# Another order in the opening of a fused attention and gated-MLP kernel, and its transposing transfers issued apart

## The chip, the cores and the metric

The kernel runs on one core of a Trainium2 chip. The metric is the device time of one execution in microseconds. A core has five engines that run side by side, each with a queue of its own that is worked off in order: TensorE (PE, the matrix products, with PEld its weight loads), VectorE (DVE), ScalarE (ACT), GpSimd (POOL) and SyncE (SP, which here only issues transfers). ScalarE and GpSimd also issue some transfers. Sixteen DMA engines carry them out.

## The reference

```python
x  = A_x                                   # 2048 rows of 1024, bf16
xn = layernorm(x)                          # (x - mean) / sqrt(var + 1e-5)
q, k, v = split(xn @ wqkv)                 # 32 heads of 32
# each row attends to 8 rows: itself and 2, 4, ... 14 rows back (masked before row 0)
s  = softmax(q . k[s - 2w] * 32**-0.5) . v[s - 2w]
s  = s @ wo
b  = (silu(xn @ w1) * (xn @ w3)) @ w2      # 3584 hidden columns
out = x + s * silu(b)
```

## The kernel before

The 2048 rows are four chunks of 512 (`CH`), handled in two blocks `b` of two chunks. Each of the large products of a block (`qkv`, the two up-projections, the down-projection, `wo`) is done with fewer products than its size asks for: sums and differences of blocks of operands are formed on VectorE (`xn_sums`, `qkv_sums`, `w_sums`, `w2_sums`, `wo_sums`), multiplied on TensorE, and put together from PSUM by ScalarE (copies, helper `cp`, line 447) and VectorE (additions, helper `tt`, line 442). Every product goes through `mm` (line 433). Two smaller helpers for products of 256 columns are at lines 1008 and 1267.

The code does not issue instructions in the order in which it is written. Each step becomes an `Op` of a `Plan` with an engine, cells that it reads and writes, and a cost. `Plan.depend` derives who follows whom from the cells, `Plan.limits` gives each a due time, counted back from the fixed order of TensorE, and `Plan.simulate` goes through time with a cost model and lets each engine take, of the steps that are ready, the one that is due first. The result is the order of instructions on each queue. `plan.nudge` shifts single due times by hand (the name of a step and its occurrence), and `plan.rows` fixes the order of the opening by hand: one list each for VectorE, ScalarE and SP. The waits in the program come from the tiles that instructions touch, not from the cells.

**Opening.** TensorE first does twelve products on zeros (line 406). SP loads the four row groups of chunk 0 (`x0_0` to `x0_3`, 256 KB each), those of chunk 1 (`x1_...`), and the weights of `q` and `k` in halves (`wqkv0_0` in two pieces `a` and `b`, `wqkv0_1`, `wqkv1_0`, `wqkv1_1`; 1 MB a half). VectorE takes the statistics of each group (`bn`, `ba`, lines 512 and 515), ScalarE the root (`sq`, line 517), VectorE the reciprocal (`rc`) and the normalising (`ts`, line 520). Group 2 of chunk 0 takes its statistics on ScalarE instead (`ln_mix`, lines 553 to 562). TensorE then transposes a normalised group by eight products with a unit matrix (`ln_tp`, line 585; called `tp` below), and ScalarE copies them to `xT` (line 592). In `rows0`, `q` of chunk 0 is computed for each row group as soon as it is there (`part`), with products on zeros between (`idle_mm`, line 572). `k` follows (`qkv_first` with `mid`): four products groups on `wqkv1_0`, with the transposing of a group of chunk 1 after each.

**Chunks 2 and 3.** Their rows are normalised on ScalarE alone in `mlp_down(0)` (`ln_act`: `mean`, `var`, `sq`, then `nrm` at line 544) and transposed by DMA: `ln_td` (line 601) issues one transposing transfer for each row group, eight in all, from ScalarE's queue.

**Around them, in `mlp_down`.** `pa`, `pb` and `pe` are PSUM banks of the three streams. ScalarE makes the gates (`gsilu`, step `dg`, line 450), the copies `dfork`, `dsu`, `dsp` and, at 256 columns, `dq21`, `dq5`, `dq2`. VectorE adds with `dq12`, `dq22`, `dsb`, `dsa`. TensorE may write a bank `pe[g]` in the second half only after `dsp` has copied it. `dsb` reads the product that then follows.

**Attention** runs on VectorE as filling work beside the products: `qk`, `qa`, `qb`, `qc`, then a softmax (`z`, `tr`, `zd`; the exponential on ScalarE at line 866 with a table load of its own), then `pv`, `pa`. Attention of a chunk lasts over many product steps.

Of the kernel before, what the change touches and what calls it, by code (L numbers as in the profile page):

```python
# [14 lines left out]
PE, DVE, ACT, POOL, SP = range(5)  # L15
# [39 lines left out]
class Plan:  # L55
# [105 lines left out]

    def hop(self, a, b):
        if a.nbytes:
            return 0.1
        if a.eng == PE:
            return 0.0 if b.eng == PE else 0.25
        return 0.05
# [25 lines left out]
    def simulate(self):  # L193
        ops = self.ops
        free = [0.0] * 5
        ready = [[] for _ in range(5)]
        pes = [o.idx for o in ops if o.eng == PE]
        pe_at = 0
        table = None
        ring = {e: [] for e in (SP, ACT, POOL)}  # L200
        now = 0.0
        for o in ops:
            o.n, o.ready = len(o.pred), 0.0
            o.start = None
        for o in ops:
            if not o.n and o.eng != PE:
                ready[o.eng].append(o.idx)
        order = []

        def landed(until):  # L210

            nonlocal now
            while True:
                heads = [r[0] for r in ring.values() if r]
                live = [h for h in heads if h[0] <= now + 1e-9]
                step = min([h[0] for h in heads if h[0] > now + 1e-9] + [until])
                if live:
                    total = sum(h[2] for h in live)
                    dt, e = min((h[1] * total / h[2], h[3].eng) for h in live)
                    end = now + dt <= step  # L220
                    dt = dt if end else step - now
                    if dt > 0.0:
                        for h in live:
                            h[1] -= dt * h[2] / total
                    if end:
                        now += dt
                        return ring[e].pop(0)[3]
                now = max(now, step)
                if step >= until:
                    return None  # L230

        def release(o, queued, data):
            for s in o.succ:
                q = ops[s]
                if (o.idx, s) in self.queued:
                    if not queued:
                        continue
                elif not data:
                    continue
                else:  # L240
                    at = o.done + self.hop(o, q)
                    if o.nbytes and q.eng != PE:
                        at += max(0.0, min(self.SPARE * (1 if o.run > 256 else 4), 0.5 * (q.limit - q.lift - at)))
                    q.ready = max(q.ready, at)
                q.n -= 1
                if not q.n and q.eng != PE:
                    ready[q.eng].append(s)

        while len(order) < len(ops):
            best = None  # L250
            for e in reversed(range(5)):
                if e == PE:
                    if pe_at == len(pes) or ops[pes[pe_at]].n:
                        continue
                    T = max(free[PE], ops[pes[pe_at]].ready)
                elif ready[e]:
                    T = max(free[e], min(ops[i].ready for i in ready[e]))
                else:
                    continue
                if best is None or T < best[0]:  # L260
                    best = T, e
            o = landed(best[0] if best else 1e9)
            if o:
                o.done = now + self.TAIL
                release(o, False, True)
                continue
            T, e = best
            if e == PE:
                o = ops[pes[pe_at]]
                pe_at += 1  # L270
            else:
                i = min((i for i in ready[e] if ops[i].ready <= T), key=lambda i: (ops[i].limit, i))
                ready[e].remove(i)
                o = ops[i]

            occ = o.occ
            if o.table and o.table != table:
                occ += 1.29
                table = o.table
            o.start = T  # L280
            free[e] = T + occ
            order.append(o)
            if o.nbytes:
                ring[e].append([T + self.LAG[e], self.work(o), self.share(o), o])
                release(o, True, False)
            else:
                o.done = T + occ + o.lat
                release(o, True, True)
        while any(ring.values()):
            o = landed(1e9)  # L290
            o.done = now + self.TAIL
        self.order = order
        return order
# [13 lines left out]
def kernel(  # L307
# [93 lines left out]
    warm = plan.pools["k2"][7][:].bitcast(BF16)  # L401
# [9 lines left out]
    def bank(name):  # L411
        return plan.slot("mm", name)
# [49 lines left out]
    def xt_cells(half, kh, st=None):  # L462
        return [("xT", half, (kh * KH + k) * 2 + q // 2, q % 2) for k in range(KH)
                for q in (range(4) if st is None else [st])]
# [101 lines left out]
    def idle_mm(n):  # L566

        ps = bank("idle")

        def emit():  # L570
            for _ in range(n):
                nc.tensor.matmul(ps.ap(), lhsT=ident[:], rhs=zero, start=True, stop=True)

        plan.op(PE, "idle", emit, [], [ps], n * MM, 0.0)
# [23 lines left out]
    def ln_td(c, st, xt):  # L598

        half = c % 2  # L600
        plan.op(ACT, f"td{c}_{st}", lambda: nc.scalar.dma_start_transpose(  # L601
            out=xT[:, half, :, st * P:(st + 1) * P], in_=xrow(xt, st)),
            [(xt, st)], xt_cells(half, 0, st) + xt_cells(half, 1, st), 1.3, 0.0, nbytes=256 * 1024, run=256)

    def qkv_load(t, pieces=1):
        wts = []
# [82 lines left out]
    def qkv_first(nm, wts, mid=None, rows=None):  # L689

        pa = [bank(f"f{nm}{j}") for j in range(4)]
        def part(st, ks=range(KH)):
            for j in range(4):
                mm(pa[j], [qkv_w(wts[0], k, j) for k in ks], [bx[0, 0][k] for k in ks], st == 0 and ks[0] == 0,
                   wk_cells(wts[0], ks) + xt_cells(0, 0, st), st=(st, 1))

        if rows:
            rows(part)
        for j in range(4):
            if mid is not None and j:  # L700
                mid(j - 1)
            if not rows:
                mm(pa[j], [qkv_w(wts[0], k, j) for k in range(KH)], bx[0, 0], True, wk_cells(wts[0]) + xt_cells(0, 0))
            dst, wr = first_at(nm, j)
            cp("fsnap", dst, pa[j].ap, [pa[j]], wr)
        for j in range(4):
            if mid is not None and j == 0:
                mid(3)
            mm(pa[j], [qkv_w(wts[1], k, j) for k in range(KH)], bx[0, 1], False, wk_cells(wts[1]) + xt_cells(0, 1))
            dst, wr = home(0, nm)(j)  # L710
            cp("fc11", dst, pa[j].ap, [pa[j]], wr)
# [815 lines left out]
    for st in range(NST):  # L1527
# [1 line left out]
    plan.op(ACT, "warm", lambda: nc.scalar.activation(out=scr[:], in_=eps_t[:], func=ACTF.Sqrt), [], [], 0.2,  # L1529
            table="sqrt")  # L1530
    plan.rows = [row.split() for row in (
# [6 lines left out]
    )]  # L1538
    plan.rank = {n: i for row in plan.rows for i, n in enumerate(row)}
    for st in range(NST):  # L1540
# [3 lines left out]
    plan.rows += [["ts1_3", f"w2s{i}"] for i in range(FH // 2)]  # L1544
    plan.rows += [["wqkv2_1", f"w2q{i}"] for i in range(5, FH // 2)]
    plan.nudge = {
# [4 lines left out]
    }  # L1551
    ln_dve(0, 0, x0)
    ln_mix(0, 2, x0)
# [2 lines left out]

    def rows0(part):
        ln_tp(0, 0, x0)
        idle_mm(4)
        part(0, (0, 1))  # L1560
        ln_tp(0, 2, x0)
        idle_mm(2)
        part(0, (2, 3))
        part(2)
        ln_tp(0, 1, x0)
        ln_tp(0, 3, x0)
        part(1)
        part(3)
# [98 lines left out]
```

## Time and profile before

| | us |
|---|---|
| runs, median of 3 (lowest to highest) | 714.8 (714.68 to 715.42) |
| the profiled execution, its own time | 714.41 |
| span of that execution | 712.6 |
| busy, of the span: PE, DVE, ACT, POOL | 704.3, 687.4, 411.2, 38.6 |

The span reaches from the first to the last instruction; what is outside it is start and end. Busy time of TensorE is counted from the start of a product to its modelled end, so that a wait shorter than the pipeline does not show. In the rows of the profile L433 is a line of the program, `mm<-xs,r` what is written and read (buffer numbers left out), `x16` how many instructions a row merges, and a bracket at the end gives the idle time of the engine ahead of the row and what ended it. "issue" means that nothing in the profile ended the wait. ACTq and SPq are the queues of ScalarE and SP.

The granted clock of TensorE in the execution is 0.999.

### The profile page before, as it was taken

The page shows a single profiled execution, that of the slowest core. Times are in us where ns is not written, and L with a number is a line of the kernel's source. Part 1 is how long each engine was busy: PE and PEld are TensorE (multiplying, and loading weights), DVE is VectorE, ACT ScalarE, POOL GpSimd, SP SyncE. Part 2 cuts the span into 40 slices and gives each one's busy share as a digit, 9 for nine tenths or more (in the row PEclk, how much of TensorE's full clock was granted, in tenths as well). Part 3 has the DMA queues.
Part 4 walks back from the last instruction along what each step waited for, and adds up shares of the span by engine and source line. Part 5 has one row for each costly group of instructions (what it writes and reads, how often), then busy time and mean ns, then how long its engine had stood idle before and what let it go on. Part 6 is the DMA issues. An engine that isn't in the chain of part 4 may idle for free.

```text
span 712.6 us, 9970 instructions
## 1 busy us (share of the span) xinstructions
PE 704.3 (99%) x3634; PEld 369.1 (52%) x3634; DVE 687.4 (96%) x959; ACT 411.2 (58%) x762; POOL 38.6 (5%) x78
## 2 busy tenths in 40 slices
PE   8999999999999999999999999999999999999997
PEld 5655555555555544644555555544555554465443
DVE  7998999999999999999999999998999999999967
ACT  7744466668766796622635355668665764431333
POOL 0010111001200000000100000000000000100000
PEclk9999999999999999999999999999999999999999
DMA  9879987567865768797724569979656654646633
GB/s 326 324 282 324 316 301 237 207 209 265 258 210 174 244 219 210 208 277 267 249 86 168 178 189 354 326 251 287 218 168 233 183 169 156 188 135 230 228 142 104
DMA packets 132241, 162.13 MB, mean 228 GB/s; under 512 B 13280, under 2 KB 109152, under 8 KB 126688
## 3 DMA queue, kind: packets, MB, share of 16 engines
q1 hardware_dynamic: 117776, 127.35, 55.5%
q0 software_dynamic: 5824, 31.99, 12.0%
q10 hardware_dynamic: 8592, 2.16, 1.7%
q8 instruction: 28, 0.46, 0.3%
q14 instruction: 21, 0.17, 0.1%
HBM read 112.72 MB, written 38.27 MB: 212 GB/s over the span
## 4 chain that ended last, share of the span: by engine, by line
PE 56%; DVE 1%; ACT 1%; ACTq 1%; issue 0%; DVEq 0%
PE mm L433 51%; PE mm L1008 3%; PE mm L1267 2%; DVE r L442 1%; ACTq L601 1%; ACT k L447 0%; ACT L866 0%; ACT L450 0%; ACT h_sb L450 0%; ACT att L866 0%; DVEq L1662 0%; ACTq L866 0%; DVEq L442 0%
## 5 line engine op out<-in xcount | busy, mean ns | idle before, releaser
L433 PEld LDWEIGHTS <-r 128*128 128x128 bf16 (+1 forms) x2064 | 217.9, 108 | 195.9 <-issue 1.5
L433 PE MATMUL mm<-xs,r 128*128 128x512 f16 x1056 | 251.4, 379 | 0.2 <-ACT k L447 0.2
L433 PE MATMUL mm<-xT,r 128*128 128x512 bf16 (+1 forms) x1008 | 232.3, 369 | 0.9 <-ACT k L447 0.5
L447 ACT COPY k<-mm 128x512 f32<-128x512 f32 (+1 forms) x256 | 132.9, 535 | 58.8 <-PE mm L433 44.0
L433 PE MATMUL mm<-r,h_sb 128*128 128x512 bf16 (+1 forms) x704 | 154.1, 379 | 1.1 <-ACT k L447 1.1
L433 PEld LDWEIGHTS <-h_sb 128*128 128x128 f16 (+1 forms) x800 | 78.3, 98 | 94.8 <-issue 1.3
L442 DVE TENSOR_TENSOR att<-att 128x1024 bf16<-128x1024 bf16 (+6 forms) x176 | 104.7, 610 | 3.7 <-ACT att L866 2.5
L447 ACT COPY mm<-mm 128x512 f32<-128x512 f32 (+1 forms) x120 | 62.1, 520 | 55.9 <-PE mm L433 41.7
L442 DVE TENSOR_TENSOR att<-qo,kT 128x2048 bf16<-128x2048 bf16 x64 | 78.0, 1226 | 3.7 <-ACT kT L447 2.9
L450 ACT ACTIVATE k<-k 128x512 bf16<-128x512 f32 x56 | 33.2, 625 | 62.9 <-DVE k L442 62.9
L442 DVE TENSOR_TENSOR att<-E,vT 128x2048 bf16<-128x2048 bf16 x56 | 66.9, 1223 | 0.0
L442 DVE TENSOR_TENSOR r<-r,r 128x256 f16<-128x256 f16 (+7 forms) x99 | 64.0, 663 | 0.7 <-PE mm L433 0.4
L442 DVE TENSOR_TENSOR h_sb<-mm,k 128x1024 bf16<-128x1024 f32 (+1 forms) x56 | 61.2, 1108 | 0.1
L1008 PEld LDWEIGHTS <-r 128*128 128x128 f16 x392 | 38.3, 98 | 28.3
L450 ACT ACTIVATE h_sb<-mm 128x512 bf16<-128x512 f32 x60 | 35.9, 601 | 18.9 <-PE mm L433 18.8
L442 DVE TENSOR_TENSOR k<-mm,k 128x1024 f32<-128x1024 f32 (+1 forms) x44 | 45.2, 1029 | 1.1 <-PE mm L433 1.0
L1008 PE MATMUL mm<-xT,r 128*128 128x256 f16 x224 | 42.8, 273 | 0.0
L447 ACT CAST k<-mm 128x512 bf16<-128x512 f32 x56 | 32.5, 586 | 15.6 <-PE mm L433 15.4
L442 DVE TENSOR_TENSOR h_sb<-h_sb 128x1024 f16<-128x1024 bf16 (+3 forms) x51 | 39.3, 804 | 0.1
L442 DVE TENSOR_TENSOR qo<-qo,att 128x2048 bf16<-128x2048 bf16 x32 | 39.2, 1224 | 0.1
L442 DVE TENSOR_TENSOR r<-r 128x1024 f16<-128x1024 bf16 (+2 forms) x64 | 36.8, 581 | 0.0
L442 DVE TENSOR_TENSOR h_sb<-h_sb,k 128x2048 bf16<-128x2048 bf16 x28 | 34.3, 1225 | 0.3 <-ACT k L447 0.3
(107 smaller groups left out, 511.7 us busy)
## 6 DMA issues: line engine op xcount, KB each, us to landing
r<-in_B_w_dram SPq DMA_DIRECT2D x42, 512.0 KB, 4.9
s_dram<-r POOLq DMA_DIRECT2D x14, 1024.0 KB, 5.4
r<-t_dram SPq DMA_DIRECT2D x16, 896.0 KB, 6.9
r<-s_dram SPq DMA_DIRECT2D x14, 1024.0 KB, 5.5
r<-in_A_wqkv_dram SPq DMA_DIRECT2D x11, 1024.0 KB, 7.7
r<-in_B_w_dram SPq DMA_DIRECT2D x12, 896.0 KB, 4.8
h_sb<-in_B_w_dram SPq DMA_DIRECT2D x14, 512.0 KB, 11.1
t_dram<-h_sb POOLq DMA_DIRECT2D x7, 1024.0 KB, 6.9
```

The costliest lines, as they stand in the source:

```text
L433: nc.tensor.matmul(cut(ps.ap()), lhsT=lhs[k](), rhs=cut(rhs[k]()), start=(first and k == 0), stop=(last and k == n - 1), skip_group_check= ...
L442: plan.op(DVE, name, lambda: fn(out=o(), in0=a(), in1=b()), rd, wr, occ, 0.08, late=late)
L447: plan.op(ACT, name, lambda: nc.scalar.copy(out=o(), in_=a()), rd, wr, occ, 0.11)
L450: plan.op(ACT, name, lambda: nc.scalar.activation(out=o(), in_=a(), func=ACTF.Silu), rd, wr, occ, 0.11, table="silu")
L601: plan.op(ACT, f"td{c}_{st}", lambda: nc.scalar.dma_start_transpose(out=xT[:, half, :, st * P:(st + 1) * P], in_=xrow(xt, st)), [(xt, st)] ...
L1008: nc.tensor.matmul(ps.ap()[:, h * 256:(h + 1) * 256], lhsT=lhs[k](), rhs=rhs[k](), start=first and k == 0, stop=False, skip_group_check=True)
L1267: nc.tensor.matmul(ps.ap()[:, col * 256:(col + 1) * 256], lhsT=lhs[k](), rhs=r()[:, k, :], start=first and k == 0, stop=False, skip_group_ ...
```

## The change

Three parts.

1. The planner: a transposing transfer now also writes a cell `"turned"`, so that the planner puts the eight one behind the other. `hop` lets such a transfer follow 1.4 us before the planner's landing of the last, and the planner's spare time for landings is left out there.
2. The opening: `x0_3` is loaded ahead of the weights, `x1_1` ahead of `wqkv0_1`; two products on zeros instead of six; `part(2)` in two halves around `tp0_1`; VectorE's first statistics of group 1 go ahead of the reciprocal of group 0, and `qs2` (one of the sums of weights) goes from behind group 0 to behind `ts1_1`; ScalarE's roots and copies are ordered to match. In `qkv_first`, the first transposing of chunk 1 goes ahead of the first products of `k`, the next two ahead of the third and the fourth.
3. Other nudges, which shift due times of steps throughout.

```diff
     def hop(self, a, b):
         if a.nbytes:
-            return 0.1
+            return -1.4 if a.run == b.run == 256 and a.eng == b.eng == ACT else 0.1
...
-                    if o.nbytes and q.eng != PE:
+                    if o.nbytes and q.eng != PE and at > o.done:
...
         plan.op(ACT, f"td{c}_{st}", lambda: nc.scalar.dma_start_transpose(
             out=xT[:, half, :, st * P:(st + 1) * P], in_=xrow(xt, st)),
-            [(xt, st)], xt_cells(half, 0, st) + xt_cells(half, 1, st), 1.3, 0.0, nbytes=256 * 1024, run=256)
+            [(xt, st)], xt_cells(half, 0, st) + xt_cells(half, 1, st) + ["turned"], 1.3, 0.0, nbytes=256 * 1024, run=256)
...
         for j in range(4):
-            if mid is not None and j:
-                mid(j - 1)
+            if mid is not None and j != 1:
+                mid(max(j - 1, 0))
...
     plan.rows = [row.split() for row in (
-        "bn0_0_0 bn0_0_1 ba0_0 rc0_0 ts0_0 bn0_1_0 rc0_2 ts0_2 bn0_1_1 bn0_3_0 ba0_1 bn0_3_1 rc0_1 ba0_3 ts0_1 rc0_3 ts0_3 "
-        "bn1_0_0 bn1_0_1 ba1_0 qs2 bn1_1_0 bn1_1_1 rc1_0 ts1_0 ba1_1 bn1_2_0 bn1_2_1 rc1_1 ts1_1 ba1_2 bn1_3_0 rc1_2 ts1_2 "
-        "bn1_3_1 ba1_3 rc1_3 ts1_3 qs0 qs1 xs0 qs3 xs1",
-        "warm mean0_2 sq0_0 var0_2 sq0_2 xT0_0_0 xT0_0_1 xT0_2_0 sq0_1 xT0_2_1 sq0_3 xT0_1_0 xT0_3_0 xT0_1_1 xT0_3_1 fsnap "
+        "bn0_0_0 bn0_0_1 ba0_0 bn0_1_0 rc0_0 ts0_0 bn0_1_1 rc0_2 ba0_1 ts0_2 bn0_3_0 bn0_3_1 rc0_1 ba0_3 ts0_1 rc0_3 ts0_3 "
+        "bn1_0_0 bn1_0_1 ba1_0 bn1_1_0 bn1_1_1 rc1_0 ba1_1 ts1_0 bn1_2_0 rc1_1 bn1_2_1 ts1_1 qs2 ba1_2 bn1_3_0 bn1_3_1 "
+        "rc1_2 ba1_3 ts1_2 rc1_3 ts1_3 qs0 qs1 xs0 qs3 xs1",
+        "warm mean0_2 sq0_0 var0_2 sq0_2 xT0_0_0 sq0_1 xT0_0_1 xT0_2_0 sq0_3 xT0_2_1 xT0_1_0 xT0_1_1 xT0_3_0 xT0_3_1 fsnap "
         "sq1_0 sq1_1 sq1_2 sq1_3",
-        "x0_0 x0_2 x0_1 wqkv0_0a x0_3 wqkv0_0b x1_0 wqkv0_1 x1_1 x1_2 wqkv1_0 x1_3 wqkv1_1",
+        "x0_0 x0_2 x0_1 x0_3 wqkv0_0a wqkv0_0b x1_0 x1_1 wqkv0_1 x1_2 wqkv1_0 x1_3 wqkv1_1",
     )]
...
     plan.nudge = {
-        ("wu0", 2): 10.01, ("w3.4", 0): -20.17, ("wu0", 4): 8.99, ("ws0", 5): -6.56, ("uq12", 6): 9.09, ("ws1",
...
+        ("wu0", 2): 10.01, ("w3.4", 0): -16.78, ("wu0", 4): 8.98, ("ws0", 5): -12.22, ("uq12", 6): 9.09, ("ws1",
...
     def rows0(part):
         ln_tp(0, 0, x0)
-        idle_mm(4)
+        idle_mm(2)
         part(0, (0, 1))
         ln_tp(0, 2, x0)
-        idle_mm(2)
         part(0, (2, 3))
-        part(2)
+        part(2, (0, 1))
         ln_tp(0, 1, x0)
+        part(2, (2, 3))
         ln_tp(0, 3, x0)
```

6 rows, old and new, of the table table are left out of this document.

## The prediction

> **What bounds the kernel now.** I read the busy shares first, then the stages, then the waits. In the stage rows the columns are: stretch, its length, the busy time and count of PE, PEld, DVE, ACT and POOL, the granted clock, the DMA share and GB/s.
>
> ```profile
> PE 704.3 (99%) x3634; PEld 369.1 (52%) x3634; DVE 687.4 (96%) x959; ACT 411.2 (58%) x762; POOL 38.6 (5%) x78
> ```
> ```profile
> 66.00:260.00 194.00, 194.00 (x998) 99.83 (x997) 193.55 (x300) 132.25 (x254) 20.63 (x38) 1.00 0.72 243
> 260.00:303.00 43.00, 41.87 (x243) 23.65 (x242) 42.87 (x59) 30.52 (x50) 0.99 (x2) 1.00 0.79 216
> 303.00:484.00 181.00, 181.00 (x872) 94.64 (x870) 178.98 (x229) 90.08 (x164) 6.15 (x12) 1.00 0.74 235
> ...
> 497.00:685.00 188.00, 188.00 (x979) 95.74 (x978) 186.67 (x222) 93.54 (x175) 5.46 (x10) 1.00 0.59 191
> ```
>
> TensorE is full nearly everywhere, and VectorE is just as full: 193.55 of 194 us from 66 to 260, 178.98 of 181 from 303 to 484. Time can come only from the few holes, and where VectorE has none, TensorE cannot run ahead for long. The waits name the holes.
>
> ```profile
> PE mm L433 <- ACT k L447: 1.8, 3, 1.1
> ```
> ```profile
> ACT L450 <- issue: 5.8, 1, 5.8
> ACT r L544 <- issue: 5.5, 1, 5.5
> ```
>
> TensorE waits 1.8 us for copies of ScalarE (line 447), and ScalarE twice sits idle over 5 us with no releaser, only "issue". The transposing transfers (line 601) explain that. Of the eight issues the shortest, the median and the longest, in ns, and then ScalarE at the longest wait of TensorE (ACTq is its queue, which issues):
>
> ```profile
> L601 ACTq DMA_TRANSPOSE xT<-r x8: 1247/1600/6474, 264.6 to 301.4; - x8
> ```
> ```profile
> 292.17 0.38 ACT L447 COPY k<-mm 128x256 f32<-128x256 f32 x1
> ...
> 294.84 1.25 ACTq L601 DMA_TRANSPOSE xT<-r  x1
> 294.97 0.38 ACT L447 COPY k<-mm 128x256 f32<-128x256 f32 x1
> 296.18 3.65 ACTq L601 DMA_TRANSPOSE xT<-r  x1
> 299.88 0.58 ACT L447 COPY k<-mm 128x512 f32<-128x512 f32 x1 [4.53 <-PE mm L1267]
> ```
> ```profile
> 297.69 0.93 PE L1267 MATMUL mm<-r,xs 128*128 128x256 f16 x7
> 298.45 0.93 PE L1267 MATMUL mm<-r,xT 128*128 128x256 f16 x7
> 300.51 3.83 PE L433 MATMUL mm<-r,h_sb 128*128 128x512 bf16 x17 [1.13 <-ACT k L447]
> ```
> ```profile
> 303.73 0.69 DVE L442 TENSOR_TENSOR k<-mm,k 128x512 f32<-128x512 f32 x1 [0.76 <-PE mm L433]
> ```
>
> An issue alone takes 1.25 us; one right behind another takes 3.65, and the copy `dsp` queued behind it starts at 299.88, when the queue is free again. TensorE needs that copy before it may overwrite the bank. Seven products of 256 columns take 0.76 us from start to start (297.69 to 298.45), so the next product was due at 299.21 and came at 300.51: **1.30 us** lost. VectorE then stands 0.76 us at its next product-fed addition (`dsb`).
>
> **The change part by part.**
>
> *Transposes one by one.* The new cell "turned" binds each to the one before it in the planner only; no instruction gets a wait from it. In the changed order of ScalarE the first of the second four stands ahead of the last two 128x256 copies, the second behind them, the third behind the four `dsp`, the last behind the first gate. So the second follows the first by two copies and their waits. It is still ahead of `dsp`. ScalarE's queue reaches the first at about 292.3 (the copy ahead of it, `dq5`, started at 292.17, and the queue runs ahead of its engine), and the second at about 295, where the second small copy ran (294.97). From 294.84 to the end of the following issue, 299.83, the first needed 4.99 us to make room: 292.3 + 5.0 = 297.3. The `dsp` copy then starts at about 297.3, ends at 297.9, and the bank is free before 299.21. Gain on TensorE 1.30; on VectorE 0.76, because it goes on without the hole. The price of the first transpose ahead of two copies that TensorE needs through VectorE is between nothing and 1.25 us; I take nothing, as those copies were held by the normalising pass (line 544) before, which now stands ahead of them.
>
> *Opening.* All of VectorE's and TensorE's work up to 17.8 us ends in a wait for a load of weights:
>
> ```profile
> 5.55 0.16 DVE L519 RECIPROCAL small<-small 128x1 f32<-128x1 f32 x1 [0.49 <-ACT small L517]
> ...
> 6.21 0.69 DVE L512 BATCH_NORM_STATS2 small<-r 128x6 f32<-128x512 bf16 x1
> ```
> ```profile
> 6.81 1.03 PE L572 MATMUL mm<-E,ident 128*128 128x512 bf16 x4
> 7.67 0.65 PE L433 MATMUL mm<-xT,r 128*128 128x128 bf16 x8
> ...
> 16.69 0.81 PE L433 MATMUL mm<-xT,r 128*128 128x512 bf16 x3
> 17.82 1.08 PE L433 MATMUL mm<-xT,r 128*128 128x512 bf16 x4 [0.32 <-DMA r<-in_A_wqkv_dram]
> ...
> 20.06 0.61 PE L585 MATMUL mm<-ident,r 128*128 128x128 bf16 x8
> 20.51 0.82 PE L433 MATMUL mm<-xT,r 128*128 128x512 bf16 x3
> ```
> ```profile
> 2.00:16.00 14.00, 13.55 (x123) 9.22 (x122) 11.65 (x28) 10.32 (x25) 0.15 (x2) 1.00 0.99 363
> ```
>
> SP's loads ahead of the end of `wqkv1_0` stay the same 4.75 MiB (seven of x at 256 KB, three MiB of weights), on DMA engines that are full (a share of 0.99), so I keep 17.82 for it. Four products on zeros less are 4 x 0.215 (6.81 to 7.67) = 0.86 us of TensorE, hidden under loads: `wqkv0_0a` now follows `x0_3`, and the second part of `q` needs `wqkv0_0b`, whose place is unchanged. They are worth nothing by themselves. VectorE's first statistics of `x0_1` (0.6 us; a row of one lasts 0.69, pipelined) go into the hole of 0.49 from 5.06 (0.49 ahead of 5.55) and stand ahead of `rc0_0` and `ts0_0`, which everything on TensorE waits for. The trace shows only that `x0_1` was there at 6.21; so these two come between 0.1 (rows there at 5.06) and 1.26 us later; I take 0.45. `x1_1` ahead of `wqkv0_1` delays these weights by 256 KB, 0.7 us at 363 GB/s. TensorE ended `q` at 17.34 (16.69 and three products of 0.215); with fewer zeros and rows earlier I put it at 16.85, and between 16.7 and 17.34. What counts is behind it: the first transposing by products of chunk 1 (`tp1_0`) now stands ahead of the products on `wqkv1_0`, so it runs inside the wait before 17.82. It costs 20.06 to 20.51, **0.45 us**, which leaves the path; TensorE would be ready at 17.3, with 0.52 to spare, and even from 17.34 it would just be in time. On VectorE, `qs1` overwrites chunk 1 only after the last such transposing, so it gains the same 0.45. Nothing stands between that and the point where attention starts:
>
> ```profile
> 65.94 1.23 DVE L442 TENSOR_TENSOR att<-qo,kT 128x2048 bf16<-128x2048 bf16 x1 [2.91 <-ACT kT L447]
> ```
>
> VectorE waits there for a copy that TensorE feeds, so both carry 0.45 to 299.
>
> *Nudges.* Between 18 and 66 only one exchange of ScalarE's copies, at 44, is new. VectorE's order from 66 to 484 differs by exchanges of neighbours, one product of attention put off from 260 to 281, and the sums of 323 to 333 in another order. In 259 to 262 a product with the gate now follows copies that end close ahead of it: I count 0.1 us of idle VectorE, between 0 and 0.3. Two loads change places with a neighbour. All are behind full engines and cost nothing, if their readers are not late.
>
> *Where the lead is spent.* TensorE is then 1.75 us early at 303 and VectorE 0.45 + 0.76 - 0.1 = 1.11. From there to 484 VectorE has no hole left, and at 484 ScalarE's exponential stops TensorE:
>
> ```profile
> 482.89 1.27 DVE L442 TENSOR_TENSOR att<-att 128x128 f32<-128x128 f32 x3
> ```
> ```profile
> 483.81 0.58 ACT L447 CAST k<-mm 128x512 bf16<-128x512 f32 x1 [0.28 <-PE mm L433]
> 484.42 1.28 ACT L866 ACT_TABLE_LOAD   x1
> ```
> ```profile
> 489.25 1.02 PE L433 MATMUL mm<-xT,r 128*128 128x512 bf16 x4 [0.50 <-ACT k L447]
> ```
>
> Its operand leaves VectorE at 484.16 (482.89 + 1.27), and ScalarE was free at 484.39. With ScalarE 1.75 early and VectorE 1.11, VectorE decides: 483.05 instead of 484.39, 1.34 early. The other 0.4 us of TensorE's lead turn into a longer wait before 489. Behind it TensorE has no hole to 685, so 1.34 reaches the end.
>
> **Sum.** 0.45 (opening) + 0.76 (VectorE's hole) - 0.1 (nudges) + 0.23 (margin at 484) = 1.34. The profiled execution took 714.41 (span 712.6, 1.8 outside): 713.07. The median of the runs, 714.8, is 0.39 above it, so 713.46; I say **713.4**. Were TensorE alone the bound, 1.75 would be saved: 713.05.
>
> **The rivals.**
>
> *The weights land earlier.* By bytes, 363 GB/s over 14 us are 5.08 MB by 16.0, and 4.98 MB stand up to the end of `wqkv1_0`; TensorE got it at 17.82. So a late piece, not the bytes, made the last microsecond, and it may fall elsewhere. TensorE would start at 17.3: 0.5 more, **712.9**. Against it: the queue's order is nearly the same.
>
> *The transposes still block.* If an issue is long because the shared DMA engines are loaded, spacing the issues does nothing, the `dsp` copy is late again and VectorE's hole stays: only 0.45 is left, 713.96 and with the 0.39 **714.4**. The DMA busy share in tenths, 294 to 308 in 40 slices, speaks for both:
>
> ```profile
> DMA  0000058799999999999999799999999999990009
> ```
>
> From 295.75 on the engines were busy with another load, so the first transpose may have been slow for that alone. But up to there nothing moved: issued at 292.3, the first finds them free before the second comes. The Trainium skill, "DMA: Bandwidth & Descriptors", section "Issuing engines are not separate DMA queues", says that the queues share 16 engines and an issue is usually small beside its transfer. By that rule a queue of transposes would not hold ScalarE and spacing would gain only the opening. The 3.65 against 1.25 us speak against it.
>
> *Slower: TensorE's clock falls to half in the opening*, since the products on zeros that keep it busy are fewer. Before it is warm its first twelve products take 4.74 us, 0.4 each against 0.215 later:
>
> ```profile
> 1.22 4.74 PE L406 MATMUL mm<-k 128*128 128x512 bf16 x12 [1.22 <-DVE k L403]
> ```
>
> A cold stretch of T delays the opening by T/2 less the 0.52 spare. It eats all 1.34 at T = 3.7 us; one stretch as long as the first gives 715.0, two give **717.0**. Against it: the holes that I find are up to 0.9 us (5.96, the end of the row above, to 6.8), and the 1.3 us at 299 left the granted clock at 1.00. The Trainium skill, "TensorE: Matmul & The Clock Gate", section "What's actually happening", wants an idle window of about 3.4 us for a fall; by it this rival would be dead.
>
> **How the numbers follow.** Forecast 0.50, early weights 0.20, still blocked 0.16, cold clock 0.07; 0.07 is left for stalls that I do not see in the reordered stretches, mostly a few tenths slower. A measurement of this kernel tells about 0.2% from no change, 1.43 us: the line is at 713.37, through the middle of the forecast (itself 713.0 to 713.9). So faster is 0.20 and half of 0.50, 0.45; slower 0.09, the cold clock with part of the rest; the same 0.46. The range reaches from early weights with VectorE no bound (0.95 + 1.30 saved, 712.55, rounded to 712.4) past the blocked case to 715.0, one cold stretch.
>
> **What would show it.** Right: issues on line 601 near 1.25 us, above all no 3.65 ahead of `dsp`; no hole of TensorE at 299 nor of VectorE at 303; TensorE still starting on `wqkv1_0` at 17.8, with the transposing before it; a wait before 489 that has grown to about 1 us. Wrong: a TensorE hole at 289 or 296 (small copies held by the first transpose), a pace of 0.4 us a product after 6, or no growth of the wait at 489, which would free VectorE of being the bound.

## The result, and the profile after

The runs of one measurement had a median of 714.56 us before (713.97 to 715.68, 12 runs) and 712.86 us after (712.61 to 713.93, 12 runs): a ratio of **0.9979, with a 95% interval of 0.9971 to 0.9986**, so between 1.0 and 2.1 us less. The forecast was 713.4 in a range of 712.4 to 715.0. The profiled execution took 712.69 us with a span of 710.9, 1.7 less than the span of before. The interval stays below 1, so the gain is clear of noise. The prediction's line of 0.2% lies at 713.13 for this median of before: the median is beyond it, a little, and the interval reaches across it, to 713.56.

The page of the profile after: TensorE is busy 1.4 us less, and VectorE 0.6 us less.

```profile
PE 702.9 (99%) x3630; PEld 368.7 (52%) x3630; DVE 686.8 (97%) x959; ACT 412.5 (58%) x762; POOL 38.6 (5%) x78
```

The stage in which the gain was expected, with the columns as before:

```profile
260.00:303.00 43.00, 43.00 (x250) 24.21 (x248) 42.90 (x59) 32.01 (x50) 1.11 (x2) 1.00 0.88 227
```

TensorE was busy 41.87 of these 43 us before; now it has no gap. The waits of TensorE in the profile after (what waits, for what; total, times, longest):

```profile
PE mm L585 <- DVE r L520: 1.6, 1, 1.6
PE mm L406 <- DVE k L403: 1.2, 1, 1.2
PE mm L433 <- ACT k L447: 0.7, 2, 0.5
```

The wait for ScalarE's copies fell from 1.8 to 0.7 us. In the opening the wait of TensorE's first transposing for VectorE's normalising grew from 0.4 to 1.6 us, in part because the products on zeros ahead of it ended 0.4 us earlier in this trace. First the issues of the transposing transfers (shortest, median, longest in ns), then ScalarE around the second four of them, in the timeline after:

```profile
L601 ACTq DMA_TRANSPOSE xT<-r x8: 1247/1296/4752, 263.3 to 303.1; - x8
```
```profile
291.59 1.25 ACTq L601 DMA_TRANSPOSE xT<-r  x1
291.76 0.38 ACT L447 COPY k<-mm 128x256 f32<-128x256 f32 x1
...
294.24 0.37 ACT L447 COPY k<-mm 128x256 f32<-128x256 f32 x1 [0.99 <-PE mm L1267]
294.24 1.25 ACTq L601 DMA_TRANSPOSE xT<-r  x1
296.53 0.59 ACT L447 COPY k<-mm 128x512 f32<-128x512 f32 x1 [1.92 <-PE mm L1267]
```

The two issues are 2.65 us apart and take 1.25 us each; the wide copy starts at 296.53, as soon as its product is there, instead of 3.35 us later. A long issue is left (4.75 us, at 268), but there ScalarE has room. TensorE after, at the place of the old hole, and VectorE's next product-fed addition:

```profile
297.86 0.93 PE L1267 MATMUL mm<-r,xT 128*128 128x256 f16 x7
298.62 4.70 PE L433 MATMUL mm<-r,h_sb 128*128 128x512 bf16 x21
```
```profile
302.36 0.69 DVE L442 TENSOR_TENSOR k<-mm,k 128x512 f32<-128x512 f32 x1
```

From 297.86 to 298.62 are 0.76 us, the pace of seven such products: no hole. TensorE starts there 1.89 us earlier than before (300.51), VectorE 1.37 (303.73), and its bracket of 0.76 is gone. Now the opening: TensorE's first transposing before, then TensorE and VectorE after.

```profile
6.36 0.62 PE L585 MATMUL mm<-ident,r 128*128 128x128 bf16 x8 [0.39 <-DVE r L520]
```
```profile
7.14 0.62 PE L585 MATMUL mm<-ident,r 128*128 128x128 bf16 x8 [1.59 <-DVE r L520]
...
9.19 1.24 PE L433 MATMUL mm<-xT,r 128*128 128x128 bf16 x16
...
17.18 0.61 PE L585 MATMUL mm<-ident,r 128*128 128x128 bf16 x8
17.71 1.95 PE L433 MATMUL mm<-xT,r 128*128 128x512 bf16 x8
```
```profile
5.74 0.70 DVE L512 BATCH_NORM_STATS2 small<-r 128x6 f32<-128x512 bf16 x1 [0.82 <-DMA r<-in_A_x_dram]
```

The moved transposing (17.18) runs ahead of the products on the weights of `k` (17.71). But VectorE's hole was not filled; it grew from 0.49 to 0.82, since the statistics that were moved into it wait for a load. Last, the small hole at 41 that every trace has. The product behind it, before and after:

```profile
41.74 1.46 PE L433 MATMUL mm<-xs,r 128*128 128x512 f16 x6 [0.18 <-ACT k L447]
```
```profile
41.17 2.10 PE L433 MATMUL mm<-xs,r 128*128 128x512 f16 x9 [0.16 <-ACT k L447]
```

I use the start of this product as a mark. It splits a run into an **opening** (up to the mark) and a **rest** (the run's time less the mark). Before: 41.74 and 672.67; after: 41.17 and 671.52. In these two executions the opening gave 0.57 us and the rest 1.15.

### The profile page after: what moved, and what is told of

It reads as the page before. It is cut to its first block, busy times and chain, and to the rows that moved or that the text cites. A ratio compares the mean times of both kernels' runs of the same rounds, so it can differ in the third digit from the quotient of the medians.

```text
span 710.9 us, 9963 instructions
## 1 busy us (share of the span) xinstructions
PE 702.9 (99%) x3630; PEld 368.7 (52%) x3630; DVE 686.8 (97%) x959; ACT 412.5 (58%) x762; POOL 38.6 (5%) x78
## 3 DMA queue, kind: packets, MB, share of 16 engines
q10 hardware_dynamic: 8592, 2.16, 2.1%
## 4 chain that ended last, share of the span: by engine, by line
PE 97%; DVE 1%; ACT 1%; DMA 1%; issue 0%; SPq 0%; DVEq 0%; ACTq 0%
PE mm L433 87%; PE mm L1008 6%; PE mm L1267 3%; DVE r L442 1%; DMA r<-in_A_x_dram 1%; PE mm L585 1%; ACT k L447 0%; ACT L866 0%; ACT L450 0%; SPq L456 0%; DVE small L512 0%; ACT h_sb L450 0%; DVE r L520 0%; PE mm L572 0%; ACT att L866 0%
```

## The experiments

All medians stand beside the runs of before on the same chip; a ratio is given where a kernel had more than one run. "Mark" and "rest" are of the one profiled execution. Where an expectation says "at 41", it counts from the start of the hole, 0.32 to 0.35 us ahead of the mark, so its times less that start are larger by as much.

| kernel | median (runs) | before | ratio, 95% interval | mark | rest |
|---|---|---|---|---|---|
| before | 714.56 (12) | | | 41.74 | 672.67 |
| after | 712.86 (12) | 714.56 | 0.9979, 0.9971 to 0.9986 | 41.17 | 671.52 |
| e1, opening alone | 714.48 (11) | 714.68 | 0.9996, 0.9987 to 1.0005 | | |
| e2, one transposing ahead | 714.53 (11) | 714.68 | 0.9999, 0.9990 to 1.0008 | 41.34 | 672.57 |
| e3, without the opening | 713.21 (11) | 714.68 | 0.9981, 0.9972 to 0.9989 | 42.22 | 671.48 |
| e4, one transpose moved | 714.01 (11) | 714.68 | 0.9988, 0.9980 to 0.9997 | 41.66 | 672.96 |
| e5, back to back again | 714.58 (10) | 714.45 | 0.9998, 0.9989 to 1.0007 | 40.93 | 672.68 |
| e6, fuller opening | 713.33 (11) | 714.45 | 0.9984, 0.9975 to 0.9993 | 42.50 | 671.37 |
| e7, VectorE later | 715.01 (1) | 714.45 | | 42.37 | 672.64 |
| e8, no zeros | 712.91 (1) | 714.45 | | 41.34 | 671.57 |
| e9, products earlier | 712.82 (11) | 714.25 | 0.9979, 0.9970 to 0.9988 | 41.56 | 671.34 |
| e10, opening alone again | 714.75 (1) | 714.25 | | 42.18 | 672.57 |

### e5: the two transfers back to back again

The changed kernel with one move on ScalarE:

```diff
-dq21 dq5 [td3_0] dq2 dq2 [td3_1] dsp dsp dsp dsp
+dq21 dq5 dq2 dq2 [td3_0] [td3_1] dsp dsp dsp dsp
```

> The changed kernel with one instruction moved: the first of the second four transposing transfers goes behind the two small copies, so that the first two are issued back to back again, as before the change; nothing else differs. Theory that the pair alone makes the hole: the second issue takes 3 to 4 us, the wide copies wait for it, TensorE has a hole of 1.0 to 1.3 us ahead of 299 and VectorE one of 0.5 to 0.8 at 302; the wait of TensorE at 336 for VectorE goes, as TensorE is no longer ahead; 0.9 to 1.2 us slower than the changed kernel from 42 us to the end. Rival, the loaded DMA engines make the long issue: the issue takes 1.25 to 2 us here too and nothing is lost.

Its ScalarE and TensorE at the place:

```profile
293.99 0.37 ACT L447 COPY k<-mm 128x256 f32<-128x256 f32 x1 [1.16 <-PE mm L1267]
294.06 4.82 ACTq L601 DMA_TRANSPOSE xT<-r  x2
298.92 0.58 ACT L447 COPY k<-mm 128x512 f32<-128x512 f32 x1 [4.55 <-PE mm L1267]
```
```profile
297.61 0.93 PE L1267 MATMUL mm<-r,xT 128*128 128x256 f16 x7
299.55 3.61 PE L433 MATMUL mm<-r,h_sb 128*128 128x512 bf16 x16 [1.01 <-ACT k L447]
```

The row merges both issues, 4.82 us; alone on line 601 they are 1.25 and 3.53. The wide copy starts 0.04 after their end, and TensorE's hole is back: 299.55 - 297.61 - 0.76 = 1.18. The rest goes from 671.52 to 672.68, **1.16 worse**, all that the rest had gained. One point missed: TensorE's wait at 336 stays, since VectorE falls behind as well (it waits 0.57 us at 302.77 and 0.47 at 305.79).

So putting the pair back together is enough to make the hole. Loaded DMA engines alone do not make an issue long: from 294 to 296 us the DMA share was 0.09 before, where the second issue took 3.65, and 1.02 after, where it took 1.25. The packets of the transposing transfers (DMA queue q10 on the page, 2.16 MB, which is their eight times 256 KB) show more. Where the second issue came right behind the first, the first packet moved 3.4 us after the first issue (before: 294.84, then 298.25; e5: 294.06, then 297.43); where it did not, 1.6 us after it (after the change: 291.59, then 293.20). Why a pair starts so late is not shown. The Trainium skill ("DMA: Bandwidth & Descriptors", section "Issuing engines are not separate DMA queues") expects an issue to be usually small beside its transfer; the 3.53 us here, for transfers that land 6.1 and 8.6 us after their issue, do not fit that.

### e3: without the opening; e4: one transfer moved

e3 is the changed kernel with `plan.rows`, `rows0` and `mid` of before. e4 is before with one move on ScalarE, and the orders of all other engines unchanged:

```diff
-nrm3_2 dq2 nrm3_3 dq2 [td3_0] [td3_1] dsp
+nrm3_2 dq2 [td3_0] nrm3_3 dq2 [td3_1] dsp
```

> The changed kernel with the old opening: new issue order and new nudges alone. TensorE theory: the hole ahead of 300 is gone (1.30), a wait of TensorE for VectorE at 336 takes back about 0.17, so 1.1 to 1.3 saved against before, span 711.3 to 711.5. Rival, VectorE is the bound from 303 to 484 (the forecast): 0.76 - 0.1 + 0.23 = 0.9 saved, span 711.7, and the wait of TensorE before 489 grows by 0.4. Rival, the transposes still block: nothing saved.

> Before, with one instruction moved: the first of the second four transposing transfers is issued one normalising pass and one small copy earlier on ScalarE; every other engine's order is that of before. Theory that the back-to-back issue alone made the hole: no issue over 2.5 us ahead of the four wide copies, no hole of TensorE ahead of 300, TensorE 1.3 early at 303, and 1.0 to 1.3 saved at the end (TensorE theory) or 0.76 + 0.23 = 1.0 (VectorE bound, the forecast). Rival, the issue is long since the DMA engines are loaded: the second issue still takes 3 us or more and nothing is saved. Rival, the nudges make the gain: nothing or little here.

e3: the rest is 671.48, 1.19 less than before, and the same as that of the changed kernel. That is inside the 1.1 to 1.3 of the TensorE theory and above the 0.9 that the forecast makes of this part.

e4 is not what either theory said. The second issue is short (1.25 us at 294.75, only 0.27 us behind the end of the first), and the hole at 299 is gone, but another has come ahead of it. ScalarE, TensorE and VectorE of e4:

```profile
293.23 1.25 ACTq L601 DMA_TRANSPOSE xT<-r  x1
...
294.53 1.24 ACT L544 ACTIVATE r<-r,small 128x1024 bf16<-128x1024 bf16 x1 [0.67 <-issue]
294.75 1.25 ACTq L601 DMA_TRANSPOSE xT<-r  x1
```
```profile
296.08 0.92 PE L1267 MATMUL mm<-r,xT 128*128 128x256 f16 x7 [0.66 <-ACT k L447]
```
```profile
326.73 1.23 DVE L442 TENSOR_TENSOR h_sb<-r,r 128x2048 f16<-128x2048 bf16 x1 [0.82 <-DMA r<-in_A_wo_dram]
```

The first issue holds the last normalising pass by 0.67 us and with it the small copy behind; TensorE loses 0.82 there instead of 1.30. The planner's order avoids that: after the change all four passes are done when the first transfer is issued (291.59). Then VectorE waits 0.82 for the weights of `wo`, which no other trace here does, and TensorE loses 0.83 at 337. That makes this execution's rest 0.29 worse than before. The median of its runs, 0.9988 of that of before, says that most executions gained something. Why the load was late in the profiled one was not tried.

### e7: VectorE made late

Before, with one addition on VectorE done twice (`qc1`, 128x512, at 341.5).

> Before, with one addition of VectorE (128x512, 0.34 us from start to start) done twice at 341.5; the result is the same. Theory that VectorE had room there (it met TensorE's products at 344 to 346 and waited about 0.25 us in all): 0.05 to 0.15 late at 347, and nothing at the end. Rival, VectorE has no room from 303 to 484 (the forecast's picture): 0.34 late at 347 and still so at 480.

VectorE before, then in e7; each time the addition behind the doubled one and one 5 to 6 us later, and for e7 the additions ahead of the exponential, which stood at 482.89 before:

```profile
341.88 0.43 DVE L442 TENSOR_TENSOR xT<-xs,xT 128x512 f16<-128x512 f16 x1
...
347.28 0.68 DVE L442 TENSOR_TENSOR h_sb<-h_sb 128x1024 bf16<-128x1024 bf16 x1
```
```profile
342.88 0.42 DVE L442 TENSOR_TENSOR xT<-xs,xT 128x512 f16<-128x512 f16 x1
...
348.02 0.69 DVE L442 TENSOR_TENSOR h_sb<-h_sb 128x1024 bf16<-128x1024 bf16 x1
...
483.49 1.27 DVE L442 TENSOR_TENSOR att<-att 128x128 f32<-128x128 f32 x3
```

Ahead of it e7 runs 0.54 behind before (338.61 against 338.07, its opening). Behind the doubled addition it is 1.00, so that cost 0.46, not 0.34. Five microseconds later it is 0.74: **0.26 us were made good in waits that VectorE had there anyway**. At 483.49 it is 0.60, no later than TensorE (482.49 against 481.89), so 0.40 of the 0.46 were made good ahead of the exponential. The margin of 0.23 that the prediction found there did not hide it: VectorE's operand (483.49 + 1.27) is again 0.25 ahead of ScalarE, which is free at 485.01. TensorE's product at 489 is 0.61 late (489.86 against 489.25), where TensorE was 0.53 late at 338 already (339.03 against 338.50), and the rest is 672.64, as in before. VectorE was not the bound of this stretch. This is one execution.

### e1, e2 and e10: the opening alone

e1 and e10 are before with the whole second part of the change. e2 is before with one edit:

```diff
-            if mid is not None and j:
-                mid(j - 1)
+            if mid is not None and j != 1:
+                mid(max(j - 1, 0))
```

> Before, with the whole new opening (row lists, loads, zeros, transposing by products put ahead) and the old issue order of the transposing transfers and old nudges. TensorE theory: the opening is worth what TensorE shows at 23 us, 0.55 us, and all of it reaches the end; the hole of 1.3 us ahead of 300 and VectorE's 0.76 at 303 stay as they are, so the ratio is 0.9992 and the span 712.05. Rival, VectorE is the bound from 303 on (the forecast): the same 0.45 to 0.55, as both engines carry it. Rival, the new opening only wins by luck of one late DMA packet: between 0 and 1.1 us off TensorE's start on the second half of the weights of k.

> Before, with one edit alone: the first transposing by products of chunk 1 stands ahead of the products on the first half of the weights of k. Theory that this move is the whole gain of the opening: TensorE ended q at 17.34, 0.45 more is 17.79, still ahead of the weights (17.82), so 0.42 to 0.45 us saved, span 712.15 to 712.2. Rival, the gain comes of the rows' and loads' order and of fewer products on zeros: 0.0 to 0.1 saved, and TensorE starts on the weights of k 0.4 later, at 18.2.

> The new opening with the rest of before, once more, since the first profiled execution was disturbed for reasons of its own. If what stands behind 42 us is the same in every execution of one order, then the time less TensorE's start at the hole of 41 is 673.0 as in before, whatever the opening does; TensorE gets there between 40.3 and 42.2, as in the other traces with this opening.

The profiled execution of e1 took 4284 us, against 713.36 to 714.83 in its other ten; its trace is not read. e1 and e2 cannot be told from before, but their intervals (about 0.6 us to either side) hold the expected 0.4 to 0.55 as well. The traces tell more. TensorE in e2 at the place where before waited for weights, and in e3, which has the old opening, where it starts on the second piece of the weights of `q`:

```profile
17.47 0.61 PE L585 MATMUL mm<-ident,r 128*128 128x128 bf16 x8
17.92 0.39 PE L433 MATMUL mm<-xT,r 128*128 128x512 bf16 x1
```
```profile
10.24 1.69 PE L433 MATMUL mm<-xT,r 128*128 128x128 bf16 x24 [0.55 <-DMA r<-in_A_wqkv_dram]
```

In e2 TensorE goes from the transposing (0.45 long) into the products of `k` without a wait: the weights of `k` had landed at 16.8, ahead of 17.47, so there was no wait in which it could hide. That load ends late in some executions only. Its sixteen parts land one by one. Before, fifteen were there at 16.66 and the last at 17.78; the last part came 0.9 to 1.5 us behind the fifteenth in five of the eleven traces (before, after, e5, e7, e9), and at most 0.53 us behind in the other six. So the wait on which 0.45 us of the forecast rest is one late part of a load, and six of the eleven traces do not have it. Each trace also has one 16 KB packet of the instruction queue that takes 1.0 to 1.1 us on a DMA engine at about that time (before: from 15.52); that it holds up the late part is a guess.

What came late in e2, e3 and e8 is the second piece of the weights of `q`: TensorE waits for it and starts on it at 9.36, 10.24 and 9.51. In the changed kernel it lands just when TensorE gets there (9.19), and in e5 and e10 TensorE gets there after it (9.04 and 10.27). In these three `q` ends 10.04 us behind TensorE's first transposing (7.14 to 17.18, 7.03 to 17.07, 8.27 to 18.31), which waits for VectorE. So the load that sets the end of `q` is not the same in all executions.

e10 shows the price of the moved statistics. Its VectorE and TensorE:

```profile
6.87 0.69 DVE L512 BATCH_NORM_STATS2 small<-r 128x6 f32<-128x512 bf16 x1 [1.75 <-DMA r<-in_A_x_dram]
```
```profile
8.27 0.62 PE L585 MATMUL mm<-ident,r 128*128 128x128 bf16 x8 [1.74 <-DVE r L520]
```

The second rows (`x0_1`) landed late, and since their statistics now stand ahead of the first rows' normalising, everything waited. e10 reached the mark at 42.18, later than before, and its rest is 672.57, as expected.

The rest repeats so well (672.57 to 672.68 in five traces with the old hole at 299, 671.48 to 671.57 in three without) that I estimate a run's opening as its time less its kernel's rest. I took 672.61 (the mean of before, e2, e7 and e10) and 671.52. For the old opening (92 runs: before and e3) the mean is 41.96 with a standard deviation of 0.50; for the new (34 runs: after, e1, e5, e8, e10) 41.71 and 0.49. That makes **the opening worth about 0.25 us**, with a standard error of 0.10 if all runs were alike. They are not quite: the mean for before alone is 42.12, 41.94 and 41.68 in three measurements (33, 21 and 15 runs), and e3, with the old opening, comes out 0.29 below before of its own measurement. So the 0.25 is an estimate from pooled runs, and a gain of the opening is not shown beyond that.

### e8: no products on zeros behind the first transposing

The changed kernel with `idle_mm(2)` left out.

> The changed kernel without its last two products on zeros in the opening (those that only keep TensorE busy behind the first transposing; the twelve at the start stay). Theory that they cost and bring nothing: TensorE waits instead, a product takes the same time from 8 us on, and TensorE's shift at 41 against the changed kernel is what the landing of the second piece of the weights of q gives, within 0.1. Rival, the clock falls: products of 128x512 at a pace of 0.4 instead of 0.215 for some microseconds after 8, 0.5 us or more lost.

Counted by its pace, TensorE idles 0.72 us from 7.45 and 0.34 from 9.17. In the window from 8 to 16 us the granted clock (third figure from the end) stays full:

```profile
8.00:16.00 8.00, 7.65 (x98) 6.82 (x99) 7.08 (x19) 6.66 (x17) 0.00 (x0) 1.00 1.05 392
```

The mark is 41.34, 0.17 later than that of the changed kernel, and the products on the second piece of weights start 0.32 later (9.51 against 9.19). The expectation allowed these two 0.1 apart and they are 0.15 apart; but the mark lost less than the late piece alone would give, so in this one execution the zeros were worth nothing. In e10 TensorE even stood idle 1.74 us ahead of 8.27, and its next eight products took 0.45 us from start to start, as always. The Trainium skill ("TensorE: Matmul & The Clock Gate", section "What's actually happening") asks for an idle window of about 3.4 us; these holes are shorter, and no fall was seen.

### e6 and e9: can the opening be bettered?

Both are the changed kernel in a forced order. e6 puts the first rows' normalising ahead of the second rows' statistics again, one root of ScalarE behind a copy, some products of `q` ahead of those that wait for the second piece of weights, and two transposings ahead of `k`. e9 keeps one transposing ahead of `k` as in the changed kernel, does the rest as e6, and besides transposes the third rows ahead of TensorE's first products and moves two roots of ScalarE behind copies. Both also have, at 336, on VectorE:

```diff
-qs0 qs2 os0 qs1
+os0 qs0 qs2 qs1
```

> The changed kernel, forced in order, nothing left out: statistics of the second 128 rows behind the normalising of the first; the products of the third 128 rows with the first piece of the weights of q ahead of those that need the second piece; two transposings of chunk 1 instead of one ahead of the products on the weights of k; and at 336 the sum that TensorE waits for ahead of two longer ones. Theory that the second piece of the weights of q (landed 9.1 to 10.2 in the traces so far) and 8 us of products behind it set the end of q, and the weights of k seldom do: about 0.4 to 0.5 us less than the changed kernel at 41, whatever the loads do, 0.1 more at 336; in all ratio 0.9970 to 0.9975 against before. Rival, the wait for the weights of k sets the opening in every run: 0.45 as well, but only if these come in time. Rival, VectorE's later statistics delay the rows of chunk 0: nothing, or up to 0.5 slower than the changed kernel.

> The changed kernel in another forced order, nothing left out: as in the fuller opening, VectorE normalises the first rows ahead of the second rows' statistics; TensorE transposes the third rows ahead of its first products, and does the third rows' products with the first piece of the weights of q ahead of those that need the second piece; ScalarE's two small square roots go behind the copies that TensorE waits for; at 336 the sum that TensorE waits for goes first. Theory that the landing of the second piece of the weights of q and 8.0 us of TensorE behind it set the opening: the end of q comes 7.5 us after that landing, so 0.3 to 0.5 less at 41 for the same landing, and 0.15 less behind 42 (time less TensorE's start at 41: 671.7); median 712.2 to 712.5. Rival, the other half of the weights of q or those of k bind next: only 0.15 to 0.25 less than the changed kernel.

e6 missed. TensorE in e6:

```profile
8.96 0.72 PE L433 MATMUL mm<-xT,r 128*128 128x128 bf16 x8 [1.62 <-DMA r<-in_A_wqkv_dram]
...
10.58 1.15 PE L433 MATMUL mm<-xT,r 128*128 128x128 bf16 x16 [0.45 <-ACT xT L592]
```

Here the first piece of weights was late already, and the third rows' transposing stood behind the products that wait for it, so nothing was there to fill the wait. e9 mends that order. Its median, 712.82, is that of the changed kernel and not the 712.2 to 712.5 of the theory; its runs lie closer together: 712.65 to 713.26, against 712.61 to 713.93. In its trace `q` ended 7.9 us after the landing of the second piece (9.36) and not 7.5, held at 10.3 by VectorE, and then the next load was waited for:

```profile
18.09 1.95 PE L433 MATMUL mm<-xT,r 128*128 128x512 bf16 x8 [0.25 <-DMA r<-in_A_wqkv_dram]
```

So the rival's mechanism is seen in this trace: the next load binds. The opening's gain over the changed kernel that it names, 0.15 to 0.25, is too small for these runs to show. The rest of both, 671.37 and 671.34, is 0.15 to 0.18 below that of the changed kernel: the exchange on VectorE took away a wait of 0.17 of TensorE (below; in e9 its product groups there start 1.73 apart, at 335.26 and 336.99), and all of it reached the end. No version here beats the changed kernel by more than the measurement can tell.

## Why the prediction was right, and where not

**The hole at 299** (1.30 on TensorE, 0.76 on VectorE): right, in its cause and its sizes. TensorE is 1.89 us ahead there, 0.57 of it from the opening; VectorE is 1.37 ahead; and e5 brings the hole back. The rival "the transposes still block" did not come about at these copies. One step on the way was wrong, without harm to the sum: that the first transfer needs 4.99 us "to make room". By it the second issue could not have ended before 296.58 (291.59 + 4.99); it ended at 295.49, and in e4 the second followed the first by 1.52 us, start to start, and was as short.

**Nothing for the first transfer ahead of the small copies**: right for this order. e4 shows that the price, 0.82, is real where normalising passes stand behind the issue.

**The nudges, 0.1 on VectorE at 259 to 262**: not seen. VectorE is 1.37 ahead at 302.36, and the opening's 0.57 with the hole's 0.76 make 1.33; the forecast had 1.11.

**"From there to 484 VectorE has no hole left"**: this step failed, and with it "VectorE decides" at 484 and the growth of the wait at 489. VectorE before, then after, where it meets products of TensorE:

```profile
343.95 0.69 DVE L442 TENSOR_TENSOR att<-att 128x512 f32<-128x512 f32 x1
344.74 0.69 DVE L442 TENSOR_TENSOR h_sb<-mm,k 128x512 bf16<-128x512 f32 x1
345.35 0.41 DVE L442 TENSOR_TENSOR att<-att 128x256 f32<-128x256 f32 x1
```
```profile
342.51 0.69 DVE L442 TENSOR_TENSOR att<-att 128x512 f32<-128x512 f32 x1
343.11 0.69 DVE L442 TENSOR_TENSOR h_sb<-mm,k 128x512 bf16<-128x512 f32 x1
343.71 0.42 DVE L442 TENSOR_TENSOR att<-att 128x256 f32<-128x256 f32 x1
```

From the first to the second start are 0.79 us before and 0.60 after. The operations last 0.69, so the wait is only 0.10 beyond the end of the one before and gets no bracket; but such operations, when none waits, follow one another every 0.60. Counted by starts, VectorE waited 0.25 us for TensorE here (its lead grows from 1.44 at 338 to 1.70 at 347). With TensorE early, these waits go. The one place where VectorE did take something from TensorE is ahead of that. VectorE and TensorE after:

```profile
336.03 0.69 DVE L442 TENSOR_TENSOR h_sb<-qo 128x1024 f16<-128x1024 bf16 x1
```
```profile
334.88 1.89 PE L433 MATMUL mm<-r,qo 128*128 128x512 bf16 x8
336.77 1.90 PE L433 MATMUL mm<-h_sb 128*128 128x512 f16 x8
```

The same two groups before, with no wait between them:

```profile
336.77 1.89 PE L433 MATMUL mm<-r,qo 128*128 128x512 bf16 x8
338.50 1.89 PE L433 MATMUL mm<-h_sb 128*128 128x512 f16 x8
```

The second product group starts 1.89 after the first, where eight products take 1.73 (8 x 0.216, and so before): a wait of 0.17 for the sum that ends at 336.72. In place of the forecast's margin and VectorE's hole, the rest gained 1.30 - 0.17 = 1.13 (1.15 in the profile) instead of 0.89. Behind 347 both engines carry the same lead, and the wait at 489 is as before, here 0.51:

```profile
482.71 1.28 ACT L866 ACT_TABLE_LOAD   x1
```
```profile
487.54 0.81 PE L433 MATMUL mm<-xT,r 128*128 128x512 bf16 x3 [0.51 <-ACT k L447]
```

Both are 1.71 earlier than before (484.42 and 489.25), which is the difference of the spans. The exponential's operand leaves VectorE at 482.44 and ScalarE is free at 482.69: ScalarE came last, as before, and not VectorE. The text had named this as the sign "which would free VectorE of being the bound". e7 (VectorE 0.46 late, and the rest as before) and e9 (TensorE's wait at 336 taken away, all of it gained) show it by experiment. The forecast's gain of the rest, 0.89, fell short by 0.2 to 0.3.

**The opening, 0.45**: 0.57 between the two profiled executions, by the mechanism named, but with 0.08 to spare at 17.7 instead of 0.52. Both executions are among those in which the last part of the weights of `k` came late; over all runs about 0.25 is left, as an estimate. "I keep 17.82" was the mistake: a landing in one trace was taken for a constant, and this load landed between 16.8 and 18.4 in the eleven traces. The VectorE hole of 0.49 did not fill (I took 0.45 us of delay; it was 0.78 at TensorE's first transposing, 7.14 against 6.36), and when the second rows land late it delays the first transposing by 1.1 us more (e10, 8.27). The rival of early weights is right in that the landing moves by more than the gain; its 0.5 more did not come.

**The cold clock**: refuted for the holes that these kernels have (e8 and e10). The early zeros were worth nothing, as forecast. Its prices were added up a little low: with the 4.74 us of the first stretch they come to 715.3 and 717.6.

**The sum**: 1.34 forecast; 1.70 in the runs (interval 1.0 to 2.1). Counted by parts, 1.13 for the rest and 0.25 for the opening make 1.4: so some of the 1.70 may be the luck of the openings in those runs. That the forecast came this close is luck in part too: its rest was too small and its opening, by this estimate, too large. This is argued from the pooled runs, not shown.

## What to carry to other kernels

Judge whether a second engine is full by the distance of starts against the usual pace, not by brackets: waits shorter than an engine's pipeline overlap show in neither the busy share nor the idle time, and they are slack. A wait for a load in one trace is a sample: compare several traces before work is moved into it, and split the time at a mark that all traces share, so that a noisy opening does not hide what the rest does. Look at what stands right behind a transposing transfer on an engine that also computes: here a second one in a row held the copies by over 3 us, other work between the two took that away, and placed ahead of late work (e4) an issue cost TensorE 0.82 us.

## What was not expected of the hardware

- A transposing transfer issued 2.65 us after the last took 1.25 us of ScalarE's queue; right behind it, 3.53 (e5). The distance is not all: 0.27 us after the end of the one before an issue took 1.25 (e4), 0.14 us after it 4.75 and 1.32 us after it 2.04 (both in the first four of the changed kernel). What sets the length stays open.
- One load of 1 MB had fifteen of its sixteen parts landed at 16.66 and the last at 17.78 (before); in e3 the last came 0.01 us behind the fifteenth.
- The same opening reached its mark at 41.66 to 42.37 in four traces (before, e3, e4, e7), while each kernel's rest behind it repeated within 0.1 us in all but one (e4). In these traces nearly all the spread of the times lies in the opening.
